# Filler products of 256 columns, and filler in two later gaps of a planned attention and expert kernel

## The chip, the cores and the metric

The kernel runs on one core of one Trainium2 chip. The metric is the device time of one execution in microseconds (us). Three unprofiled runs of the kernel before are shown, and one more execution that carried the profile.

## What is computed

The reference first does attention over pooled keys and values: k and v are averaged over groups of 8 rows, so each of the 64 (batch, head) pairs has 72 keys, and 576 queries attend to them. The 4608 rows that come out go through a feed-forward layer whose activation is a quotient of polynomials.

```python
scores = scale * q @ k_pooled.T          # per batch and head, 576 x 72
attn = softmax(scores)
x = (attn @ v_pooled).transpose(0, 2, 1, 3).reshape(4608, 512)
h = x @ w_in                             # 512 -> 2048
g = (a0 + a1*h + a2*h**2 + a3*h**3) / (1 + |b0|*|h| + |b1|*h**2 + 1e-6)
out = g @ w_out                          # 2048 -> 512
```

The two weight matrices arrive in 64 bits. Products of matrices are made in several passes over high and low parts of the operands (fp32r), to keep fp32 accuracy.

## The kernel before, in words

The rows are cut into 18 blocks of 256 (index i), the hidden dimension into 8 slices of 256 (index u). For a pair (i, u) there is a first product `ph{i}_{u}` = x times a slice of w_in (24 matmuls of 256 columns, L257 in every row, since all planned operations are issued from that line), a quotient on ScalarE, VectorE and GpSimd (tiles `t`, `w`, `r`, `rp`, `gh`, `gl`), and a second product into `po` (matmuls of 512 columns). Attention for block i is made shortly before its first pair: transposes of q (`pq`), scores (`ps`), transposes of the probabilities (`pm`, `pr`), values (`pv`). Keys and values of a batch are pooled first: `pk` and `pl` are transposes of pooled keys, `pvs` and `pvr` sum the values of batches 0 and 1 by products with the identity. So the first 110 us hold loads, weight conversion, pooling and attention together, and from then on the work is a stream of `ph` and `po`.

What each engine does when is not written out by hand. `Plan.add` (L120) records each operation with a planned duration and its dependencies. `Plan.solve` (L153) plays all engines forward by these planned durations and gives each operation a planned start and end, and the order of all operations. `Plan.issue` (L238) emits them in that order. Nothing of the planned times is in the program except the order, and one more thing: the filler.

TensorE executes its queue in order. In `issue` (L247 to L255), ahead of each TensorE operation planned before `steady`, products of the identity with itself (`filler`, 128 x 128, fp32r) are emitted to occupy the time for which the plan leaves TensorE idle. They write to a PSUM bank of their own, `plan.idle` (L852), and nothing reads them; these are the rows of L253, `idle<-identr`. How many are emitted is counted against planned times: one per 0.215 us where the plan is before `WARM` = 8.6 us, one per 0.1 us later. `steady` is the planned start of the second marked product on `plan.idle` (L855). That bank then goes to another tile. The number of filler products is fixed when the program is built, and each of them is executed, whether the engine is late at that point or not.

PSUM has 8 banks, and a ring of 8 tiles (tag `ps`) is allotted to `pk`, `ps`, `ph`, `rp`, `po` and the others in the order in which they are first written (`Buf.real`, L93). The first instruction that writes a new tile waits until the last reader of the bank's tile before it is done. Two such places matter here. The bank that `pk1` gets (keys of batch 1) held `ph0_2`, whose last reader is the VectorE operation `t<-t,abn,ph`. The bank that `ph0_3` gets held `rp0_2`, whose last reader is VectorE's `t<-rp,t`.

All loads and stores are issued by SyncE, in planned order, on one hardware queue: keys and values of batches 0 and 1 go to tiles called `early`, queries to `q`, raw weights to `rwin` and `rwout`. The two small loads of 64 KB that end the values of batch 1 (`early<-in_v_dram`) feed `pvr1`, the 16 matmuls `pvr<-early,fourfold` of batch 1.

Of the kernel before, what the change touches and what calls it, by code (L numbers as in the profile page):

```python
# [8 lines left out]
F32 = mybir.dt.float32  # L9
# [90 lines left out]
class Plan:  # L100
    LAT = 0.07

    BEGIN = {"sp": 0.8, "pe": 1.7, "pool": 1.3, "dve": 1.5, "act": 1.5}
    WARM = 8.6

    LOOK = 0.02

# [45 lines left out]
    def solve(self):  # L153
# [15 lines left out]
        while done < len(self.ops):  # L169
# [44 lines left out]
            op.start, op.end = t, t + op.cost  # L214
            if op.eng == "pe" and t < self.WARM:
                op.end = t + 2 * op.cost
# [21 lines left out]
    def issue(self):  # L238
        for op in self.order:
            for b in op.bufs:  # L240
                b.it = None
        engines = {"sp": self.nc.sync, "act": self.nc.scalar, "actq": self.nc.scalar,
                   "dve": self.nc.vector, "pool": self.nc.gpsimd, "pe": self.nc.tensor}
        value = lambda v: v.ap() if isinstance(v, Lazy) else v
        free, steady = None, [o.start for o in self.order if self.idle.tile in o.bufs][-1]
        for op in self.order:
            if op.eng == "pe" and op.start <= steady:  # L247

                while free is not None:
                    free += 0.1 if free > self.WARM else 0.215  # L250
                    if free > op.start:
                        break
                    self.nc.tensor.matmul(self.idle.ap(), lhsT=self.filler, rhs=self.filler,  # L253
                                          start=True, stop=True)
                free = op.end  # L255
            for name, args, kw in op.calls:
                getattr(engines[op.eng], name)(*map(value, args),  # L257
                                               **{k: value(v) for k, v in kw.items()})
# [17 lines left out]
def tile_pooled_attention_then_rational_moe(  # L276
# [20 lines left out]
    P = 128  # L297
# [13 lines left out]
    plan = Plan(nc)  # L311
# [16 lines left out]
    def new(where, tag, shape, dtype, name):  # L328
        return plan.tile(*pools[where], shape, dtype, tag, name)

    def bank(name, shape):
        return new("ps", "ps", shape, F32, name)
# [5 lines left out]
    def pe(ns, calls, claims=(), after=()):  # L338
        return plan.add("pe", ns / 1000, calls, claims=claims, after=after)

    def mm(out, lhsT, rhs, start, stop):
        return "matmul", (out,), dict(lhsT=lhsT, rhs=rhs, start=start, stop=stop)

    def dma(kbytes, dst, src, eng="sp", issue=0.48, early=60.0, after=()):
        plan.add(eng, issue, [("dma_start", (dst, src), {})], bytes=kbytes * 1024, early=early,
                 after=after)
# [7 lines left out]
    ident = identr.bitcast(F32)  # L354
# [494 lines left out]
    for i in range(2):  # L849
        plan.add("pool", 0.5, [("memset", (kpT[i], 0.0), {})], port=True)  # L850

    plan.idle = bank("idle", [P, P])  # L852
    pe(0, [mm(plan.idle, ident, ident, True, True)])
    plan.now = HEAD + 6.0
    plan.add("pe", 0, [mm(plan.idle, ident, ident, True, True)], early=0.0)  # L855
    plan.now = 0.0
    for g in range(4):
        small("tensor_copy", out=fourfold[:, g * 32:(g + 1) * 32], in_=ident[:2 * REM, :2 * REM])
# [60 lines left out]
```

## Time and profile before

| | |
|---|---|
| Runs without a profile | 958.46, 959.37, 956.49 us (median 958.46) |
| The profiled execution | 961.21 us |
| Its span, first to last instruction | 959.5 us |
| Mean granted TensorE clock | 0.996 |
| Filler products executed | 101 (128 columns), 2.12 to 42.3 us |

The span is the time between the first and the last instruction in the trace; the execution's time holds 1.7 us around it. TensorE (PE in the rows) is busy in almost all of the span. A row of the timeline gives the start in us, the time from the first start to the last end of consecutive equal instructions, the engine, the line, the operation with the names of its tiles, and the count; what stands in brackets is idle time of the engine before it and what ended it. Ends of matmuls overlap the next start, so the distance between starts is what a product costs. An fp32 product is recorded as two matmuls.

### The profile page before, as it was taken

To read this page: it belongs to the slowest core of one execution; us is meant where nothing else is said; L and a number is where in the kernel's file an instruction comes from. 1 tells how busy PE (TensorE), PEld (TensorE's weight loads), DVE (VectorE), ACT (ScalarE), POOL (GpSimd) and SP (SyncE) were. 2 spreads that over 40 slices of the span, in tenths; PEclk is the share of its full clock that TensorE was granted. 3 is DMA by queue.
4 is the path that set the end of the run, shared out by engine and by line. 5 is a ranking of instruction groups with operands and counts; after the bars stand their busy time and mean duration, and the time that the engine had idled before them with its cause. 6 is when DMAs were issued, how large, how long until landed. Compare 5 with 4: busy or idle time off the path is not lost.

```text
span 959.5 us, 17276 instructions
## 1 busy us (share of the span) xinstructions
PE 945.0 (98%) x6233; PEld 858.9 (90%) x6233; DVE 780.7 (81%) x1346; ACT 695.0 (72%) x1180; POOL 510.9 (53%) x445
## 2 busy tenths in 40 slices
PE   9989999999999999999999999999999999999998
PEld 8978899988998999999999899999999889999996
DVE  4798988888888878788888897979787878787664
ACT  2787888858676867776776786777867676767674
POOL 3566557756446645454644484447545564544353
PEclk9999999999999999999999999999999999999999
DMA  9967110155133213123303240225121411102000
GB/s 304 333 241 238 32 40 1 45 138 132 44 73 70 64 31 80 22 46 66 107 14 63 58 123 3 38 64 115 34 32 41 96 38 28 40 3 43 1 23 23
DMA packets 156692, 71.65 MB, mean 75 GB/s; under 512 B 133952, under 2 KB 133952, under 8 KB 156608
## 3 DMA queue, kind: packets, MB, share of 16 engines
q1 hardware_dynamic: 156608, 70.56, 28.5%
q8 instruction: 49, 0.80, 0.4%
q14 instruction: 35, 0.29, 0.1%
HBM read 50.60 MB, written 12.58 MB: 66 GB/s over the span
## 4 chain that ended last, share of the span: by engine, by line
PE 92%; DVE 4%; DMA 1%; POOL 1%; ACT 1%; issue 1%; SPq 0%; POOLq 0%; DVEq 0%
PE ph L257 40%; PE po L257 39%; PE pv L257 4%; PE ps L257 4%; PE idle L253 2%; DVE t L257 1%; DMA st_v<-in_v_dram 1%; PE pvs L257 1%; PE pr L257 1%; PE pvr L257 0%; DVE rp L257 0%; PE pk L257 0%; DVE sm L257 0%; PE pq L257 0%; POOL st_v L257 0%
## 5 line engine op out<-in xcount | busy, mean ns | idle before, releaser
L257 PEld LDWEIGHTS ph<-x,win 128*128 128x128 f32 x3264 | 484.1, 189 | 63.6 <-ACT r L257 2.5
L257 PE MATMUL ph<-x,win 128*128 128x256 f32 x3264 | 502.7, 282 | 2.9 <-DVE t L257 2.3
L257 PE MATMUL po<-wout,gh 128*128 128x512 f32 x1152 | 358.9, 398 | 0.0
L257 POOL TENSOR_TENSOR w<-w,r 128x512 f32<-128x512 f32 (+1 forms) x145 | 190.6, 1314 | 257.8 <-ACT r L257 240.7
L257 POOL TENSOR_TENSOR gl<-t,gh 128x512 fp32r<-128x512 f32 (+1 forms) x145 | 192.6, 1328 | 97.7 <-ACT gh L257 97.3
L257 PEld LDWEIGHTS po<-wout,gh 128*128 128x128 f32 x1152 | 182.6, 189 | 7.0
L257 PE MATMUL po<-wout,gl 128*128 128x512 f32 x576 | 181.6, 396 | 0.5 <-POOL gl L257 0.5
L257 DVE SCALAR_TENSOR_TENSOR t<-t,abn,rp 128x512 f32<-128x512 f32 (+1 forms) x145 | 107.0, 738 | 50.8 <-ACT rp L257 48.0
L257 DVE TENSOR_TENSOR t<-t,ph 128x512 f32<-128x512 f32 (+1 forms) x145 | 98.0, 676 | 61.1 <-ACT t L257 59.2
L257 ACT ACTIVATE w<-ph 128x512 f32<-128x512 f32 (+1 forms) x145 | 86.1, 594 | 71.6 <-PE ph L257 67.2
L257 ACT ACTIVATE rp<-w,cbias 128x512 f32<-128x512 f32 (+1 forms) x145 | 100.0, 690 | 45.5 <-POOL w L257 43.3
L257 ACT ACTIVATE r<-w,abn 128x512 f32<-128x512 f32 (+1 forms) x145 | 118.2, 815 | 10.6 <-POOL gl L257 4.4
L257 ACT ACTIVATE t<-ph,abn 128x512 f32<-128x512 f32 (+1 forms) x145 | 111.0, 766 | 18.7 <-PE ph L257 14.7
L257 DVE SCALAR_TENSOR_TENSOR t<-t,abn,ph 128x512 f32<-128x512 f32 (+1 forms) x145 | 107.6, 743 | 6.3 <-ACT w L257 1.3
L257 ACT CAST gh<-t 128x512 fp32r<-128x512 f32 (+1 forms) x145 | 88.5, 610 | 22.8 <-DVE t L257 19.9
L257 DVE SCALAR_TENSOR_TENSOR t<-rp,t 128x512 f32<-128x512 f32 (+1 forms) x145 | 99.4, 685 | 4.2
L257 DVE SCALAR_TENSOR_TENSOR rp<-w,rp 128x512 f32<-128x512 f32 (+1 forms) x145 | 99.2, 684 | 0.1
L257 PEld LDWEIGHTS po<-wout,gl 128*128 128x128 f32 x576 | 91.1, 189 | 4.8 <-POOL gl L257 0.7
L257 ACT ACTIVATE rp<-rp 128x512 f32<-128x512 f32 (+1 forms) x145 | 84.0, 579 | 3.4 <-DVE t L257 0.5
L257 POOL TENSOR_TENSOR e<-e,sm 128x576 f32<-128x576 f32 x36 | 41.5, 1160 | 37.7 <-DVE sm L257 28.9
L257 POOL TENSOR_TENSOR st_v<-st_v 128x512 f32<-128x512 f32 (+1 forms) x36 | 36.4, 1016 | 38.8 <-DMA st_v<-in_v_dram 12.0
L257 PE MATMUL pv<-am,vm 128*128 128x256 f32 (+3 forms) x288 | 46.5, 281 | 0.5 <-DVE kpT L257 0.4
(91 smaller groups left out, 864.2 us busy)
## 6 DMA issues: line engine op xcount, KB each, us to landing
out_dram<-ob SPq DMA_DIRECT2D x17, 512.0 KB, 3.0
rwin<-in_moe_w_in_dram SPq DMA_DIRECT2D x8, 1024.0 KB, 9.9
rwout<-in_moe_w_out_dram SPq DMA_DIRECT2D x8, 1024.0 KB, 10.7
am<-e SPq DMA_DIRECT2D x224, 32.0 KB, 2.0
st_k<-in_k_dram SPq DMA_DIRECT2D x12, 512.0 KB, 4.6
st_v<-in_v_dram SPq DMA_DIRECT2D x12, 512.0 KB, 4.0
q<-in_q_dram SPq DMA_DIRECT2D x144, 32.0 KB, 2.1
st_v<-in_v_dram SPq DMA_DIRECT2D x48, 64.0 KB, 3.7
```

Source lines behind the costliest of these rows:

```text
L253: self.nc.tensor.matmul(self.idle.ap(), lhsT=self.filler, rhs=self.filler, start=True, stop=True)
L257: getattr(engines[op.eng], name)(*map(value, args), **{k: value(v) for k, v in kw.items()})
```

## The change

Four edits. The bank `idle` becomes twice as wide, and the filler's moving operand is the identity read twice (a broadcast), so one load of weights serves 256 columns instead of 128. After `WARM` the planned price of a filler is 0.12 instead of 0.1 us, which lowers their number; before it, the price stays 0.215. After `steady`, up to a planned start of 110 us, gaps are filled too, with products that write to the tile of the operation that comes next: only where this operation is the first to write its tile, the tile is F32, and the part that it writes is 128 x 128 (then 128 columns are used) or 128 x 256; the gap has to leave 0.2 us. The real operation then overwrites what they wrote.

```diff
+    FILL = 110.0
...
-            if op.eng == "pe" and op.start <= steady:
-                while free is not None:
-                    free += 0.1 if free > self.WARM else 0.215
-                    if free > op.start:
+            if op.eng == "pe" and op.start <= self.FILL:
+                to = self.idle.ap() if op.start <= steady else None
+                dst = op.calls[0][1][0]
+                if to is None and dst.tile.it is None and dst.tile.dtype == F32:
+                    to = dst.ap()
+                one = self.filler
+                if to is not None and tuple(to.shape) != (128, 128):
+                    one = one.unsqueeze(1).to_broadcast([128, 2, 128])
+                    if tuple(to.shape) not in ((128, 256), (128, 2, 128)):
+                        to = None
+                while free is not None and to is not None:
+                    free += 0.12 if free > self.WARM else 0.215
+                    if free > op.start - (0.0 if op.start <= steady else 0.2):
                         break
-                    self.nc.tensor.matmul(self.idle.ap(), lhsT=self.filler, rhs=self.filler,
-                                          start=True, stop=True)
+                    self.nc.tensor.matmul(to, lhsT=self.filler, rhs=one, start=True, stop=True)
                 free = op.end
...
-    plan.idle = bank("idle", [P, P])
-    pe(0, [mm(plan.idle, ident, ident, True, True)])
+    plan.idle = bank("idle", [P, 2, P])
+    pe(0, [mm(plan.idle[:, 0], ident, ident, True, True)])
     plan.now = HEAD + 6.0
-    plan.add("pe", 0, [mm(plan.idle, ident, ident, True, True)], early=0.0)
+    plan.add("pe", 0, [mm(plan.idle[:, 0], ident, ident, True, True)], early=0.0)
```

The planned durations, the order of operations, the allotment of banks and all transfers stay as they are.

## Rows read from the trace of the kernel before

**Rows 1.** The page's first part: busy time, share of the span, instructions.

```profile
PE 945.0 (98%) x6233; PEld 858.9 (90%) x6233; DVE 780.7 (81%) x1346; ACT 695.0 (72%) x1180; POOL 510.9 (53%) x445
```

**Rows 2.** Stretches: length, busy by engine (PE, PEld, DVE, ACT, POOL), clock, DMA, GB/s.

```profile
60.00:70.00 10.00, 6.11 (x41) 5.20 (x39) 9.88 (x18) 8.20 (x13) 6.53 (x4) 0.98 0.42 165
70.00:80.00 10.00, 9.69 (x47) 8.33 (x47) 6.34 (x14) 6.40 (x11) 4.18 (x4) 0.68 0.51 161
...
140.00:160.00 20.00, 20.00 (x130) 18.15 (x129) 16.28 (x24) 16.92 (x26) 13.78 (x9) 1.00 0.00 1
```

**Rows 3.** Timeline of TensorE, the first 50 us.

```profile
2.12 4.93 PE L253 MATMUL idle<-identr 128*128 128x128 f32 x22
...
8.26 1.12 PE L257 MATMUL pq<-identr,q 128*128 128x128 f32 x4
...
16.16 1.91 PE L257 MATMUL pvs<-early,identr 128*128 128x256 f32 x4
...
19.15 1.03 PE L257 MATMUL pvs<-early,identr 128*128 128x256 f32 x4
...
24.34 2.32 PE L253 MATMUL idle<-identr 128*128 128x128 f32 x19
26.49 0.62 PE L257 MATMUL pm<-identr,e 128*128 128x128 f32 x4
...
36.54 4.81 PE L257 MATMUL ph<-x,win 128*128 128x256 f32 x40
...
46.19 2.05 PE L257 MATMUL pvr<-early,fourfold 32*128 32x128 f32 x16
```

**Rows 4.** The chain that ended last: pieces of the late stream at full rate.

```profile
120.34 0.47 PE po L257 x2
120.80 0.47 PE ph L257 x4
```

**Rows 5.** Timeline of SyncE's queue: the last load that pvr1 needs.

```profile
29.85 0.56 SPq L257 DMA_DIRECT2D early<-in_v_dram  x1
```

**Rows 6.** That issue in the DMA view; the last number is us to landing.

```profile
early<-in_v_dram SPq DMA_DIRECT2D x1, 64.0 KB, 14.0
```

**Rows 7.** One microsecond while it waits; columns as in rows 2.

```profile
38.00:39.00 1.00, 1.00 (x11) 1.00 (x10) 0.97 (x4) 0.69 (x1) 0.00 (x0) 1.00 1.05 414
```

**Rows 8.** Timeline of TensorE around the two later gaps.

```profile
62.65 3.01 PE L257 MATMUL ph<-x,win 128*128 128x256 f32 x24
67.56 0.44 PE L257 MATMUL pk<-identr,ks 128*128 128x128 f32 x2 [1.89 <-DVE t L257]
70.31 4.60 PE L257 MATMUL ph<-x,win 128*128 128x256 f32 x20 [2.31 <-DVE t L257]
74.71 0.63 PE L257 MATMUL pk<-identr,ks 128*128 128x128 f32 x2
...
77.25 0.71 PE L257 MATMUL ps<-kpT,qT 128*64 128x144 f32 x8
```

**Rows 9.** Timeline of VectorE there.

```profile
65.30 0.41 DVE L257 TENSOR_TENSOR ks<-early 128x256 f32<-128x256 f32 x1
...
66.77 0.73 DVE L257 SCALAR_TENSOR_TENSOR t<-t,abn,ph 128x512 f32<-128x512 f32 x1
...
69.48 0.69 DVE L257 SCALAR_TENSOR_TENSOR t<-rp,t 128x512 f32<-128x512 f32 x1
```

**Rows 10.** Half microseconds at which the granted clock changes; columns as in rows 2.

```profile
69.50:70.00 0.50, 0.00 (x0) 0.00 (x0) 0.50 (x2) 0.00 (x0) 0.50 (x1) 0.67 0.00 0
...
76.00:76.50 0.50, 0.50 (x4) 0.50 (x3) 0.50 (x1) 0.40 (x2) 0.00 (x0) 0.50 0.80 307
76.50:77.00 0.50, 0.50 (x5) 0.39 (x4) 0.50 (x3) 0.11 (x1) 0.00 (x0) 1.00 0.32 90
```

**Rows 11.** Waits of SyncE's queue, first 110 us: total us, times, longest.

```profile
SPq L257 <- PE pq L257: 30.1, 4, 15.7
```

## Prediction

> **What bounds the kernel now.** I read the busy shares first: TensorE is busy in 98% of the span, VectorE in 81% [rows 1]. Then the table by stretches: late in the kernel TensorE fills each stretch, as in 140 to 160, and the poor stretches are 60 to 70 (busy 6.11 of 10 us, VectorE 9.88) and 70 to 80 (granted clock 0.68) [rows 2]. So the late stream is paced by TensorE, and a microsecond by which it starts earlier is a microsecond off the end. What the change touches lies ahead of it, in two places.
>
> The head. TensorE has a queue without gaps there, but 101 of its products are filler, and the filler shows the rate. The 22 from 2.12 on take 4.93 us (the end of the last overlaps what follows), 215 ns from start to start; the 19 from 24.34 start within 2.15 us, 113 ns [rows 3]. The profile's clock column records no step there, but the same product at half the rate says that the engine ran at 1.2 GHz first. The same four sum products take 1.91 us at 16.16 and 1.03 us at 19.15 [rows 3], so the rate doubled around 18 us. Before it TensorE had 41 fillers of 128 columns among its work, and at the end the sum products of 256 columns.
>
> The later gaps. TensorE waits 1.89 us before pk1 and 2.31 us before ph0_3 [rows 8]. The clock falls at about 69.8, after these near-empty 4.6 us, and is back at 76.5, after 6.2 us of products at 1.2 GHz [rows 8, 10]. What do the waits wait for? The pooled keys of pk1 are ready at 65.71 (65.30 plus 0.41), and it starts at 67.56, just after VectorE's read of ph0_2 ends at 67.50. ph0_3 starts at 70.31, just after the read of rp0_2 ends at 70.17 [rows 8, 9]. Both wait for the bank, not for data. That decides the second half of the change.
>
> **Part 1, the filler of 256 columns.** The plan's gaps stay, so the counts follow from the prices: gaps that held 22, 4, 8, 7, 1, 19, 7, 12, 13, 1, 7 hold 22, 4, 6, 6, 1, 16, 6, 10, 10, 0, 5. That is 86 for 101.
>
> What does one cost? ph products have 256 columns and a weight load each: 40 take 4.81 us, 120 ns [rows 3], 118 in the late stream [rows 4]. At 1.2 GHz 20 of them take 4.40 us up to the next start, 220 ns [rows 8]. Against 113 and 215 ns for 128 columns, doubling the columns costs 5 to 7 ns: the product runs beside the next load of weights. So after the rise 60 fillers of 113 ns (6.8 us) become 48 of 120 ns (5.8 us), 1.0 us less, and 3 cold ones fewer save 0.65 us.
> The Trainium skill, "TensorE: Matmul & The Clock Gate", section "Back-to-back issue gap", prices an isolated product at full rate by its columns, N/2.4 + 2.5 ns. By that 128 more columns cost 53 ns, and 48 fillers 2.5 us more instead of 1.0 less, an estimate from the page; ph at 118 to 120 ns speaks against it.
>
> What does the clock do? The trace before has no such filler, so I bound it. If nothing changes, only 1.7 us of the above are gained. If the clock rises while the first 22 fillers run or soon after, as it did at 76.5 after 6.2 us of mostly 256-column products without a break (2.12 + 6.2 = 8.3), then the stretch from 8.26 to 19.15, 10.9 us at half rate [rows 3], needs about 5.4. I take the second, because rows 8 and 10 show nearly this kind of product lifting it. An estimate with the waits for keys and values left in is that TensorE's work moves by 4.5 us at 20, and, with the thinner filler, by about 5 at 41.
>
> But this is not what arrives. pvr1 needs the last small load of batch 1's values. It is issued at 29.85 and lands 14.0 us later, at 43.85 [rows 5, 6], and the DMA engines are full meanwhile (share 1.05, 414 GB/s) [rows 7], so an earlier issue doesn't bring it sooner: what is ahead in the queue has to go through. pvr1 starts at 46.19 [rows 3], 2.3 us after the landing. TensorE works in order and would stand idle before pvr1. **Gain of the head: 2.3 us**; ends 1.7 (no earlier rise) and 5 (the loads move along). Behind it VectorE is nearly full in 60 to 70 [rows 2] and works on what pvr1 and pv1 give, so I move it by the same 2.3.
>
> **Part 2, the later gaps.** In the plan TensorE idles 2.98 us before pk1 and 2.60 before ph0_3: (2.98 - 0.2)/0.12 gives 23 products of 128 columns, (2.60 - 0.2)/0.12 gives 20 of 256. Two further gaps, before pr4 and pr5, have fp32r tiles and are left alone. The bank is now taken by the first filler instead of the first real product, so the wait for the bank moves to it: **the filler runs after the gap, not in it**. In times as before the shift:
> - pk1's bank comes free at 67.5. 23 products of 113 ns are 2.6 us, then pk1 0.2: until 70.3. This is hidden, since ph0_3's bank is free at 70.2 only; without that cover it would cost 2.6.
> - Then 20 products of 120 ns: 2.4 us on the path. Queued behind them are ph0_3 and the second part of pk1, and VectorE waits for that part.
> - The clock: TensorE is idle for 1.9 us in a row now, not 4.6 with 0.4 of work in between, so it should stay at 2.4 GHz. From 70.31 to ps at 77.25 are 6.94 us [rows 8]; at full rate the same work is 20 ph at 118 ns (2.4), pk1 (0.2), two pairs of po and a group of ph at 0.47 each (1.4) [rows 4]: 4.0. That gives back 2.9.
>
> Where the execution before had the cold stretch, the sum is 2.4 - 2.9 = -0.5; where it had none, +2.4. Ends: -2.9 (the filler is free after all) and +2.4.
>
> **Sum.** The profiled execution (span 959.5, 961.21 with what lies around it) has the cold stretch: 961.21 - 2.3 - 0.5 = 958.4. It is 2.75 above the median, about the cold stretch's price, and the three runs spread over 2.9 us, the same size. I read the runs as with and without it: 959.37 - 2.3 - 0.5 = 956.6 and 956.49 - 2.3 + 2.4 = 956.6. I forecast **956.5 us**, 0.2% under the median. A measurement of this kernel tells about 0.3% (2.9 us) from no change, so this counts as no difference.
>
> **Rivals.**
> - *Forecast:* a load bounds the head, and the second half roughly pays for itself, 955.6 to 958.5. Chance 0.47.
> - *The loads move too.* SyncE's queue waits 30 us in all for TensorE's pq [rows 11]; issued earlier, the loads might land earlier and the head gain the whole 5: 956.5 - 2.7 = 953.8. Against it: full DMA engines [rows 7]. Free later filler would give nearly the same time. Chance 0.33.
> - *The change does not do what it says*, and the clock rises no earlier: the head gains 1.7 instead of 2.3, 957.1. Chance 0.08, within the band of no difference.
> - *Slower:* the clock falls anyway in the idle time ahead of pk1. Then the filler itself runs cold. 23 x 215 ns are 4.9 us, so pk1 ends 2.4 us after ph0_3's bank is free; 20 x 220 ns are 4.4 us instead of 2.4; ph0_3's 20 products cost 4.4 instead of 2.4. That is 2.4 + 2.0 + 2.0 = 6.4 over the forecast: 962.9. It decides if the clock falls before about 67.5. For it: it fell in this place before. Against it: only 1.9 us of idle time in one piece. Chance 0.10.
> - *A filler is priced by its columns.* A po product of 512 columns takes 235 ns and a ph product of 256 takes 118 [rows 4], so 128 columns are worth 58 ns where no load of weights hides them. Before ph0_3 that is 20 x 58 = 1.2 us more, in the head 48 x 58 = 2.8, mostly in slack: 957.7 to 959. This is what the page's rule above would do. Chance 0.02.
>
> **Numbers.** Faster by over 0.3% (under 955.6): the second case and a little of the first, 0.35. Slower (over 961.3): 0.10. Within: 0.55. The range goes from 953.5 (the second case) to 959.5, where runs without an earlier cold stretch pay for the filler.
>
> **What would show it.** Fillers and real work at 110 to 120 ns from about 8 us on; if the spacing is 215 to 220 ns up to 18, part 1 failed. An idle stretch of TensorE before pvr1, ended by a DMA, with pvr1 at 43 to 44; at 41 the loads moved. The first filler of pk1 and of ph0_3 starting after VectorE's t, with idle time still ahead; fillers that start where the ph ahead of them ends would prove me wrong. Granted clock 1.00 from 60 to 80, and the ps of 77.25 some 2.5 to 3 us earlier. The forecast is wrong if the runs before do not differ by the cold stretch: then the sum holds against the profiled execution alone.

## The result and the profile after

The changed kernel takes **961.87 us** in the median of 20 executions (957.61 to 965.98); the kernel before, run 20 times beside it, 958.89 (956.13 to 961.55). The ratio is **1.0033**, with a 95% interval of 1.0018 to 1.0048: slower by 0.33%, just over the 0.3% that the prediction took as no difference. The prediction was 956.5 us in a range of 953.5 to 959.5, with 0.10 for slower. It was wrong in the time and in the sign.

The profiled execution took 965.26 us (span 963.6). Five others of the 20 are as long, so its stretches show what most of the loss looks like, not the average. The page's first part, to hold against [rows 1]:

```profile
PE 948.0 (98%) x6261; PEld 860.5 (89%) x6261; DVE 781.6 (81%) x1346; ACT 694.5 (72%) x1180; POOL 509.1 (53%) x445
```

TensorE issues 28 products more: 15 fewer in the head, 43 more in the later gaps, the numbers forecast. The shares tell nothing else, because a filler counts as busy. The stretches of the changed kernel (columns as in [rows 2]) tell more:

```profile
60.00:70.00 10.00, 8.07 (x59) 7.42 (x58) 9.87 (x16) 8.93 (x15) 6.27 (x5) 0.99 0.44 170
70.00:80.00 10.00, 10.00 (x62) 10.00 (x62) 4.53 (x9) 3.84 (x6) 4.64 (x3) 0.67 0.33 105
...
45.00:46.00 1.00, 1.00 (x10) 1.00 (x11) 0.43 (x1) 0.00 (x0) 0.15 (x1) 0.94 1.14 297
46.00:47.00 1.00, 1.00 (x6) 1.00 (x6) 0.00 (x0) 0.00 (x0) 0.00 (x0) 0.50 0.93 321
...
52.00:53.00 1.00, 1.00 (x5) 0.88 (x4) 0.95 (x3) 1.00 (x3) 0.00 (x0) 0.64 0.47 134
...
69.00:70.00 1.00, 0.69 (x5) 0.69 (x6) 0.89 (x2) 1.00 (x2) 0.98 (x2) 0.89 0.00 0
70.00:71.00 1.00, 1.00 (x7) 1.00 (x7) 1.00 (x3) 0.91 (x2) 1.00 (x1) 0.50 0.00 0
...
76.00:77.00 1.00, 1.00 (x9) 1.00 (x7) 0.00 (x0) 0.00 (x0) 0.00 (x0) 0.69 0.39 47
```

The granted clock is at half rate twice: from about 45.9 to 52.7, which is new, and from about 69.8 to 76.6, about as long as the stretch of before [rows 10] although TensorE is now "busy" throughout 70 to 80. VectorE's share there falls from 6.34 [rows 2] to 4.53; its timeline below shows that it waits for a TensorE that works on filler.

The timeline of TensorE in the changed kernel:

```profile
2.12 4.11 PE L265 MATMUL idle<-identr 128*128 128x256 f32 x22
6.34 0.44 PE L268 MATMUL pk<-identr,ks 128*128 128x128 f32 x2
...
24.18 1.43 PE L265 MATMUL idle<-identr 128*128 128x256 f32 x10
25.45 0.40 PE L268 MATMUL pv<-am,vm 128*128 128x256 f32 x2
...
32.27 4.81 PE L268 MATMUL ph<-x,win 128*128 128x256 f32 x40
...
44.87 2.82 PE L268 MATMUL pvr<-early,fourfold 32*128 32x128 f32 x16 [1.85 <-DMA early<-in_v_dram]
...
69.31 4.76 PE L265 MATMUL pk<-identr 128*128 128x128 f32 x23 [1.93 <-DVE t L268]
73.87 0.65 PE L268 MATMUL pk<-identr,ks 128*128 128x128 f32 x2
74.17 3.70 PE L265 MATMUL ph<-identr 128*128 128x256 f32 x20
77.71 2.54 PE L268 MATMUL ph<-x,win 128*128 128x256 f32 x20
...
81.80 0.71 PE L268 MATMUL ps<-kpT,qT 128*64 128x144 f32 x8
```

Read against [rows 3, 8], it gives a ledger of where the changed kernel stands relative to before:
- The rate doubles while the first 22 fillers run: they take 4.22 us to the next start, 192 ns each, and the pair of pk at 6.34 takes 0.44, as at full rate in [rows 8]. From then on the stream is ahead: the 40 products of ph start at 32.27 instead of 36.54, **4.3 us early**.
- pvr1 waits 1.85 us for its load and starts at 44.87 instead of 46.19: **1.3 us early**. Then the clock is half, and VectorE's reads that free the later banks come late: pk1's bank is free at 69.25 instead of 67.50 [rows 9], **1.75 us late**.
- The 23 fillers take 4.56 us and the 20 take 3.54. ph0_3 starts at 77.71 instead of 70.31, **7.4 us late**. It then takes 2.4 us to the next start instead of 4.4, and ps starts at 81.80 instead of 77.25, **4.55 us late**. The span is 4.1 longer.

The wait before the first filler has moved to it whole. The timeline of VectorE, the reads that free the two banks:

```profile
68.52 0.73 DVE L268 SCALAR_TENSOR_TENSOR t<-t,abn,ph 128x512 f32<-128x512 f32 x1
...
71.23 0.68 DVE L268 SCALAR_TENSOR_TENSOR t<-rp,t 128x512 f32<-128x512 f32 x1
...
80.50 0.47 DVE L268 TENSOR_SCALAR kpT<-pk 64x216 f32<-64x216 f32 x2 [4.77 <-PE pk L268]
```

The first read ends at 69.25 and the first filler starts at 69.31. ph0_3's bank is free at 71.91, while TensorE is still in pk1's fillers. The last line is who pays: VectorE stands idle for 4.77 us until the second part of pk1 is there. SyncE's queue settles the rival "the loads move too"; here the kernel before, then the changed one:

```profile
16.40 3.86 SPq L257 DMA_DIRECT2D q<-in_q_dram  x2
20.31 5.69 SPq L257 DMA_DIRECT2D early<-in_k_dram  x3
```

```profile
13.82 7.38 SPq L268 DMA_DIRECT2D q<-in_q_dram  x2
21.25 4.83 SPq L268 DMA_DIRECT2D early<-in_k_dram  x3
```

q is issued 2.6 us earlier, but the keys behind it are issued 0.9 later: the earlier start is gone with the next group of loads. pvr1's load did not come sooner: pvr1, which waits for it, starts 1.0 us after the landing of before (44.87 against 43.85, [rows 5, 6]).

**The clock of every execution** says how typical the profile is. Each has a mean granted clock over its span (as recorded, so without the slow head, which the record shows at 1.00); a half-rate stretch of 6.8 us lowers it by 0.0035 (half of 6.8 in 960). In the 20 of the changed kernel, clock and time go together:

| mean granted clock | changed kernel: executions, median us | before (104 in all): executions, median us |
|---|---|---|
| 0.992 to 0.995 | 8, 964.91 | 11, 959.11 |
| 0.996 to 0.997 | 2, 961.72 | 64, 958.80 |
| 0.998 | 7, 960.92 | 29, 958.42 |
| 0.999 | 2, 958.98 | none |
| 1.000 | 1, 957.61 | none |

Six of the 20 lie at 0.993, the profiled one with its two cold stretches among them, and take 964.77 to 965.98. The executions of before lost 0.2 to 0.8% of the clock, and it hardly showed in their time: 0.4 us between 0.996 and 0.998.

The profiled execution of before, at 961.21 us, is not typical either. Of the 124 executions run beside the others only two are longer, and the 64 with about its recorded clock (0.996 to 0.997) have a median of 958.80. So 2.4 of its microseconds are not explained by the recorded clock, and what they are was not found.

### The profile page after: what moved, and what is told of

It is laid out like the page before. It is cut to its first block, busy times and chain, and to the rows that moved or that the text cites. A ratio compares the mean times of both kernels' runs of the same rounds, so it can differ in the third digit from the quotient of the medians.

```text
span 963.6 us, 17331 instructions
## 1 busy us (share of the span) xinstructions
PE 948.0 (98%) x6261; PEld 860.5 (89%) x6261; DVE 781.6 (81%) x1346; ACT 694.5 (72%) x1180; POOL 509.1 (53%) x445
## 4 chain that ended last, share of the span: by engine, by line
PE 88%; DVE 4%; DMA 2%; SPq 2%; ACT 2%; issue 1%; DVEq 0%
PE po L268 39%; PE ph L268 39%; PE pv L268 4%; PE ps L268 3%; SPq L268 2%; DVE t L268 2%; DMA early<-in_v_dram 2%; DMA q<-in_q_dram 1%; DVE m_wout L268 1%; PE pr L268 1%; PE pk L265 0%; DVE rp L268 0%; ACT t L268 0%; PE pk L268 0%; PE ph L265 0%
```

## The experiments

Four kernels shared each set of runs of the kernel before: the first four below, the next four, the last four. "Head" is the filler up to the plan's first 37 us, "later" that ahead of pk1 and ph0_3.

**1. The head alone.**

```diff
-    FILL = 110.0
+    FILL = 37.09
```

> Edit: the 256-column filler and its lower count up to the marked product stay; the later gaps are not filled. Theory (idle time that the head's gain opens ahead of pvr1, and filler that runs after the bank wait, let the clock fall): pvr1 again starts at 44 to 45 after 1.5 to 2 us of idle time; where the clock falls there, 43 to 52 run at half rate and the head's 2 us are lost; no filler on the path before ph0_3, so 957 to 960, 1 to 4 us under the changed kernel. Rival (the later filler is harmless and the head alone makes it slower): as the changed kernel, 961 to 963.

Measured: 960.20 us (956.65 to 962.25) beside 958.68, ratio 1.0012 [1.0003, 1.0022]. Its TensorE timeline:

```profile
44.16 2.02 PE L268 MATMUL pvr<-early,fourfold 32*128 32x128 f32 x16 [1.21 <-DMA early<-in_v_dram]
...
65.50 0.44 PE L268 MATMUL pk<-identr,ks 128*128 128x128 f32 x2 [1.92 <-DVE t L268]
...
93.29 0.41 PE L268 MATMUL pr<-identr,er 128*128 128x128 f32 x2 [0.86 <-DVE t L268]
```

In this execution the head is worth what was forecast: pvr1 starts 2.0 us sooner, pk1 2.1, and the pr that stands at 96.63 before starts 3.3 sooner. But then the clock falls in a place where it did not fall in the profile of before, after waits of only 0.86 and 0.46 us (its stretches):

```profile
95.00:96.00 1.00, 1.00 (x9) 0.92 (x7) 1.00 (x3) 1.00 (x2) 1.00 (x1) 0.87 0.00 0
96.00:97.00 1.00, 1.00 (x7) 1.00 (x7) 1.00 (x2) 0.50 (x1) 0.00 (x0) 0.50 0.06 16
...
102.00:103.00 1.00, 1.00 (x6) 0.89 (x6) 0.94 (x2) 0.68 (x2) 0.32 (x1) 0.72 0.00 0
```

Seven cold microseconds take the 3.3 back, and at 103 the stream stands where before's stands. Before, then run 1:

```profile
102.96 2.44 PE L257 MATMUL ph<-x,win 128*128 128x256 f32 x20
```

```profile
102.85 2.52 PE L268 MATMUL ph<-x,win 128*128 128x256 f32 x20
```

The lead is real and is not kept here. Nor is it in most executions, as far as the clock tells: 8 of the 11 lie at 0.995 or below, of before's 104 only 11.

**2. The head's new counts with products of 128 columns** (and no later filler): is it the width or the smaller number?

```diff
-                to = self.idle.ap() if op.start <= steady else None
+                to = self.idle.ap()[:, 0] if op.start <= steady else None
```

> Edit: the lower count of filler of the change, but 128 columns as before, and no later gaps. Theory (256 columns raise the clock early): fillers at 215 ns and the rate doubling only at 15 to 18 us, pvr1 at 44.5 to 46 with little idle time ahead, 956.5 to 958.5. Rival (the count, not the columns, moved the head): clock up at 5 to 6 us as in the changed kernel, pvr1 waiting 1.5 to 2 us for its load.

Measured: 959.15 us (956.75 to 962.44), ratio 1.0006 [0.9994, 1.0018]: no difference is shown. The profile shows the rate up near 10 us and pvr1 at 43.97 after a wait of 1.08 us for its load. Here the lead is kept, to a span of 955.0 us; it is the fastest of the twelve executions. That early rate is not typical of this width, see 6; this run by itself doesn't separate width and number.

**3. The later filler alone**, with the head as before.

```diff
-                to = self.idle.ap() if op.start <= steady else None
+                to = self.idle.ap()[:, 0] if op.start <= steady else None
...
-                    free += 0.12 if free > self.WARM else 0.215
+                    free += 0.215 if free <= self.WARM else 0.1 if op.start <= steady else 0.12
```

> Edit: the head as in the kernel before (128 columns, old count), only the two later gaps filled with 23 and 20 products. Theory (the filler waits for the bank and runs after the gap): pvr1 at 46 as before without idle time ahead; idle time ahead of the filler of pk1 stays 1.8 to 2 us; ps after ph0_3 later than in the kernel before by 0 to 4.5 us depending on the clock: 959 to 963. Rival (the filler fills the gap): filler starts where ph ends at 65.7, clock 1.00 from 60 to 80, 955 to 957.

Measured: 962.27 us (956.41 to 965.87), ratio 1.0036 [1.0019, 1.0053]. **This half alone loses as much as the whole change.** Two of its twelve executions have a clock of 1.000; they took 956.41 and 957.24, and the other ten 960.68 or more.

**4. The changed kernel, with 16 fillers in pvr1's own bank ahead of pvr1**, to hold the clock through its wait.

```diff
+                if dst.tile.name == "pvr1" and dst.tile.it is None:
+                    for _ in range(16):
+                        self.nc.tensor.matmul(dst.tile.real(), lhsT=self.filler,
+                                              rhs=self.filler, start=True, stop=True)
```

> Edit: the changed kernel plus 16 filler products of 128 columns in pvr1's own bank, ahead of pvr1, where TensorE otherwise waits for the load. Theory: no fall of the clock at 43 to 46, pvr1 at 44.5 to 45 and the work behind it at full rate, 2.5 to 3.5 us won where the changed kernel has the cold stretch there, 0 where it has not: median 959 to 961; the filler before pk1 can still run cold. Rival (the clock falls for another reason or the time is lost elsewhere): 961 to 963.

Measured: 961.58 us (958.80 to 965.67), ratio 1.0029 [1.0015, 1.0043]. **The edit had no effect.** The page of its profile has as many products as the changed kernel, and none of them is a filler in pvr1's bank:

```profile
PE 943.6 (98%) x6261; PEld 856.9 (89%) x6261; DVE 781.7 (81%) x1346; ACT 694.4 (72%) x1180; POOL 509.1 (53%) x445
```

The line `to = dst.ap()` ahead of it had already given the tile its bank, so its condition `dst.tile.it is None` was never true there. So this run doesn't test what it was expected to test. It is the changed kernel once more: the loss is found again, and there is a second profile of it. In that one pvr1 waits 1.87 us and the clock is down from about 48.3 to 51.7. But this execution shows the later filler with the clock up (TensorE timeline):

```profile
68.79 2.79 PE L265 MATMUL pk<-identr 128*128 128x128 f32 x23 [1.88 <-DVE t L272]
71.41 0.41 PE L272 MATMUL pk<-identr,ks 128*128 128x128 f32 x2
71.57 2.63 PE L265 MATMUL ph<-identr 128*128 128x256 f32 x20
74.04 2.54 PE L272 MATMUL ph<-x,win 128*128 128x256 f32 x20
...
78.13 0.71 PE L272 MATMUL ps<-kpT,qT 128*64 128x144 f32 x8
```

From start to start, 23 fillers of 128 columns take 2.62 us (114 ns each), 20 of 256 take 2.47 (124 ns): the sum's prices were right within 4%, and so was the order of events. From the end of the wait ahead of pk1 to ps are 9.34 us instead of 9.69 [rows 8], 0.35 less where the forecast had 0.5 less. Still this execution took 961.49 us: after the cold stretch at 48, that wait ends 1.2 us late instead of 2.3 early. Against the 961.21 of the profiled execution before, it is the head's gain that is missing here, not the second half. And the same program, with 1.9 us of idle time ahead of pk1 in both profiles, lost the clock there in one execution and kept it in the other.

**5. Each later gap by itself.** First the 23 ahead of pk1:

```diff
-                if to is None and dst.tile.it is None and dst.tile.dtype == F32:
+                if to is None and dst.tile.it is None and dst.tile.name == "pk1":
```

> Edit: as later_only, but only the 23 products ahead of pk1. Theory: at full rate they are hidden (2.6 us until ph0_3's bank is free), at half rate they cost up to 2.3 us: 957.5 to 961. Rival (every filler product is on the path): 2.6 us over the kernel before or more, 961 to 963.

Measured: 959.41 us (954.85 to 961.06), ratio 1.0002 [0.9986, 1.0018]. Then the 20 ahead of ph0_3, the same line with that name:

> Edit: as later_only, but only the 20 products ahead of ph0_3. Theory: all 20 lie on the path, 2.4 us at full rate and up to 4.4 at half rate, and the clock falls ahead of them as before, so 2 to 4 us over the kernel before: 960.5 to 963. Rival (hidden): 958 to 959.

Measured: 962.18 us (960.17 to 964.05), ratio 1.0038 [1.0025, 1.0050], the whole loss of 3. The timeline of TensorE with the 23 only:

```profile
67.73 3.13 PE L265 MATMUL pk<-identr 128*128 128x128 f32 x23 [1.90 <-DVE t L268]
70.66 0.65 PE L268 MATMUL pk<-identr,ks 128*128 128x128 f32 x2
70.96 3.71 PE L268 MATMUL ph<-x,win 128*128 128x256 f32 x20
```

and with the 20 only:

```profile
70.31 4.63 PE L265 MATMUL ph<-identr 128*128 128x256 f32 x20 [2.22 <-DVE t L268]
74.75 3.34 PE L268 MATMUL ph<-x,win 128*128 128x256 f32 x20
```

The 23 are hidden, as forecast: ph0_3 starts at 70.96, 0.65 us after before's. The 20 are not: they stand 4.44 us on the path, at 222 ns each, because the clock is already down when they begin, as it is there before [rows 10]. Eleven of its twelve executions lie at 0.996. Three of the twelve with the 23 reached 0.999, and these took 954.85 to 955.47, the others 959.24 or more.

**6. Filling the same gaps in a bank that TensorE already holds.** The head is before's. Instead of writing to the next product's bank, 15 and 18 products of zeros are added to po's open accumulation, so that they need no bank and run in the gap:

```diff
+    HOLD = {"pk1": 15, "ph0_3": 18}
...
+                for _ in range(self.HOLD.get(first.name, 0) if first.it is None else 0):
+                    self.nc.tensor.matmul(acc.ap()[:, 0:256], lhsT=self.filler,
+                                          rhs=self.zeros[:, 0:1].to_broadcast([128, 256]),
+                                          start=False, stop=False)
+                if first.name == "po0_0_0":
+                    acc = op.calls[0][1][0]
```

> Edit: the head of the kernel before; in the two later gaps filler that needs no bank: 15 products ahead of pk1 and 18 ahead of ph0_3 of zeros, 256 columns, added into the open accumulation of po0 (so the sum is unchanged). Theory (filler behind the bank wait cannot keep the clock, filler in the gap can): filler starts where ph ends, about 65.7, pk1 and ph0_3 start when they did (67.6 and 70.3), granted clock 1.00 from 60 to 80, ps after ph0_3 near 74.3 instead of 77.25: 2 to 3 us under the kernel before, 955.5 to 957. Rival (the cold stretch there is hidden by VectorE or falls anyway): 958 to 960.

Measured: 957.76 us (954.62 to 960.35) beside 958.96, ratio 0.9991 [0.9979, 1.0002]. The timeline of TensorE:

```profile
65.37 1.84 PE L252 MATMUL po<-zeros,identr 128*128 128x256 f32 x15
67.44 0.44 PE L267 MATMUL pk<-identr,ks 128*128 128x128 f32 x2 [0.23 <-DVE t L267]
67.64 2.26 PE L252 MATMUL po<-zeros,identr 128*128 128x256 f32 x18
70.19 2.61 PE L267 MATMUL ph<-x,win 128*128 128x256 f32 x20 [0.30 <-DVE t L267]
```

The idle time is 0.23 and 0.30 us instead of 1.89 and 2.31 [rows 8]. pk1 and ph0_3 start when before's do, so the filler costs nothing. The recorded clock stays at 1.00, here where it was 0.68 [rows 2]:

```profile
70.00:80.00 10.00, 9.81 (x67) 8.31 (x67) 8.62 (x19) 7.78 (x13) 6.49 (x5) 1.00 0.72 256
```

ph0_3 takes 2.5 us instead of 4.4, and ps starts at 74.35, 2.9 us before the 77.25 of [rows 8], the 2.9 of the prediction. In six of the twelve executions the mean clock is 1.000. The products that start at 102.96 before start at 100.05 here, so in this execution the lead is not lost on the way. Yet over all of them the gain is 0.09% (0.9 us), its interval just reaching no change.

The same with the head of 2:

> Edit: the same two real gap fillings, with the head of count_only (the change's lower count, 128 columns). Theory: the head's lead of about 2 us and the gap's 2 to 3 add up unless the clock falls in the idle time ahead of pvr1 or near 95: 953.5 to 957, scattered. Rival (each lead is given back in the next wait): same as gap_po.

Measured: 957.29 us (955.35 to 959.84), ratio 0.9989 [0.9977, 1.0000]. Here the rate rose at about 18 us although the head is that of 2, and pvr1 began at 46.70 after 1.46 us of waiting. Over all profiles, one each of fourteen kernels: the five with a head of 256 columns had the full rate by 5.5 to 8 us; of the nine with one of 128, one had it at 10 and eight at 16 to 19, as in [rows 3]. So in these profiles the early rise goes with the width, not with the number.

**7. The price of the 20 with the clock held**: 6 with the change's 20 fillers ahead of ph0_3.

```diff
+                if to is None and dst.tile.it is None and dst.tile.name == "ph0_3":
+                    to = dst.ap()
```

> Edit: gap_po (clock held through both later gaps by filler that needs no bank) plus the change's 20 products ahead of ph0_3 in its own bank. Theory (they lie on the path by their own length, whatever the clock does): gap_po plus 2.0 to 2.4 us, 959.8 to 960.3. Rival (the slowdown of the 20 products was only the clock's): as gap_po, 957.3 to 958.3.

Measured: 959.37 us (958.37 to 964.91) beside 958.53, ratio 1.0016 [1.0003, 1.0029]. The timeline of TensorE:

```profile
69.19 2.66 PE L275 MATMUL ph<-identr 128*128 128x256 f32 x20 [0.21 <-DVE t L278]
71.69 2.54 PE L278 MATMUL ph<-x,win 128*128 128x256 f32 x20
```

2.50 us from start to start, and against 6 the ratios differ by 0.0025, 2.4 us, with intervals that don't overlap. The forecast's 2.4 on the path is borne out. In 5 it was 0.0038 (3.6 us), 1.2 us more than with the clock held; this difference is within the noise. Run 7 also is the second half of the forecast with its clock held, in nine of its twelve executions at 0.998 or more, and it is slower than before by 0.16%, not faster by the forecast 0.5 us.

**8. The change's head with the gaps of 6**, and then the same with every gap that it opens filled too: 7 zero products ahead of pvs1, 15 in the open pvs1 ahead of pvr1, 7 and 3 in po ahead of pr4 and pr5.

```diff
+    HOLD = {"pk1": (15, "po0_0_0"), "ph0_3": (18, "po0_0_0")}
...
+    HOLD = {"pvs1": (7, "idle"), "pvr1": (15, "pvs1"), "pk1": (15, "po0_0_0"),
+            "ph0_3": (18, "po0_0_0"), "pr4": (7, "po0_0_0"), "pr5": (3, "po0_0_0")}
```

> Edit: the change's 256-column filler in the head, and the two gaps filled with the 33 zero products instead of the change's 43. Theory (the head's lead is bounded by the load of pvr1 and lost in part where the clock falls in the idle time ahead of it): pvr1 at 44 to 46 after 1 to 2 us of idle time, median 957 to 959, more scatter than gap_po. Rival (the lead comes through): 955 to 956.

> Edit: head_gap_po plus zero products where TensorE still waits: 7 on the idle bank ahead of the first pvs1, 15 into open pvs1 ahead of pvr1, 7 and 3 into po0 ahead of pr4 and pr5. Theory (what the head wins is taken back by falls of the clock in the waits): no fall between 40 and 105, pvr1 at 44 to 46 still by its load, 954.5 to 956.5 with less scatter. Rival (the load alone decides): as head_gap_po.

Measured: 957.91 us (955.87 to 960.53), ratio 0.9989 [0.9979, 1.0000], for the first, and for the second **956.29 us (954.82 to 959.86), ratio 0.9979 [0.9967, 0.9990]**, the fastest of the study and faster than both kernels. The timeline of TensorE in the first:

```profile
44.98 2.43 PE L278 MATMUL pvr<-early,fourfold 32*128 32x128 f32 x16 [1.51 <-DMA early<-in_v_dram]
```

and in the second:

```profile
42.71 2.03 PE L255 MATMUL pvs<-zeros,identr 128*128 128x256 f32 x15
44.67 2.05 PE L279 MATMUL pvr<-early,fourfold 32*128 32x128 f32 x16
...
68.82 2.65 PE L279 MATMUL ph<-x,win 128*128 128x256 f32 x20 [0.30 <-DVE t L279]
...
73.02 0.71 PE L279 MATMUL ps<-kpT,qT 128*64 128x144 f32 x8
```

The first waits ahead of pvr1, and its clock is at half rate from 46.4 to 53.2. The second doesn't wait: pvr1 starts where the zero products end, the recorded clock is 1.00 from start to end of the stream, and eleven of its twelve executions lie at 1.000 (of before's 104 none).

**9. The gaps before pr4 and pr5 alone**, added to 6:

```diff
+    HOLD = {"pk1": (15, "po0_0_0"), "ph0_3": (18, "po0_0_0"),
+            "pr4": (7, "po0_0_0"), "pr5": (3, "po0_0_0")}
```

> Edit: gap_po plus 7 and 3 zero products into po0 ahead of pr4 and pr5, with the head of the kernel before. Theory (short waits near 95 let the clock fall in some executions): 956.5 to 957.5, 0 to 1 us under gap_po. Rival (these waits are too short to matter): as gap_po, 957.8.

Measured: 957.74 us (954.61 to 960.80), ratio 0.9992 [0.9980, 1.0003]: these two gaps by themselves bring nothing that can be seen. Between this and 8's second kernel stands only the head with its filled waits, 0.0013 or 1.2 us; the two intervals overlap, so that difference is an indication.

## Why the prediction was wrong

**Right:**
- The filler of 256 columns lifts the rate at about 5.5 to 8 us (forecast 8.3). The counts, 86, 23 and 20, were exact.
- Its price was taken as 120 ns at full rate; 24.18 to 25.45 holds ten, 127 ns, and run 4 shows 124 beside 114 for 128 columns. 128 columns more cost 10 ns; the rival that priced by columns, at 58 ns, is refuted. The Trainium skill ("TensorE: Matmul & The Clock Gate", "Back-to-back issue gap") gives a price by columns, from which 53 ns for 128 more is an estimate, for an isolated product alone, and says that in a stream of loads of weights and products both set the spacing; the trace agrees with the second.
- The bank's wait moves to the first filler, which runs after the gap (first filler at 69.31, read ended at 69.25). The 23 are hidden (run 5), the 20 cost 2.4 us where the clock holds (runs 6 and 7).
- The loads do not move (SyncE's queue), and TensorE stands idle ahead of pvr1 instead.

**The step that failed** is in part 2: "TensorE is idle for 1.9 us in a row now, not 4.6 with 0.4 of work in between, so it should stay at 2.4 GHz", which was to give back 2.9 us. I had argued that moving the wait leaves 1.9 us of idle time, and then counted that remainder as harmless. The clock fell at 69.8, just as before, after 1.93 us of idle time and half a microsecond of filler; it fell there in the profiles of runs 1, 2, 3 and 5 too, and in run 4 alone, the same program once more, it did not. In six profiles with that idle time taken away (runs 6 to 9) it never fell there. So the rival "slower", at 0.10, is the mechanism that happened. It put the decision at a fall ahead of 67.5, which was not needed: a fall during the 23 fillers is enough for the 20 to run partly cold. It priced this case at 6.4 us over the forecast, 962.9; the median is 961.87. That the two are so near is in part luck: this price still counts the head's 2.3 us as won.

Nor is it shown that the clock alone would have saved the step. Where it held, the runs disagree: two executions of run 3 at 1.000 took 956.41 and 957.24, under before's 958.68, while run 7 is 1.5 us over before.

**The second failure is "gain of the head: 2.3 us".** It was taken to be kept to the end. Run 1 measures a loss of 0.12% instead (1.2 us, 0.3 to 2.1). The profiles show two places where it goes, and both are falls of the clock. The idle time that I had forecast ahead of pvr1 was given no price, though it is of the same kind as that ahead of pk1: where it is 1.46 us or more (the changed kernel, run 4, the first of 8 and the second of 6), the clock falls 1.0 to 2.5 us after pvr1 has begun; where it is 1.08 and 1.21 (runs 1 and 2), it stays up in these profiles. And in run 1, where the lead survives, it runs into another fall at 95.7. Filling these waits took the falls away in the profile of 8's second kernel; that this is worth the 1.2 us by which it beats run 9 is an indication only. Smaller: the load that pvr1 needs landed at 43.97 to 46.70 in the six profiles where pvr1 waits for it, not always at 43.85, so even the bound was about 1 us too good.

**The third is a reading of the runs shown.** "I read the runs as with and without it", 2.9 us apart, is not borne out: of before's 104 executions none has an undisturbed clock, and those at 0.996 and at 0.998 differ by 0.4 us. Nor does taking away the cold stretch give 2.9 in the median: run 6 does it, ps is 2.9 us earlier, and 0.9 is left. The premise that a microsecond by which the late stream starts earlier is a microsecond off the end is not what failed: in all thirteen profiles the shift at 102.96 against before comes out in the span within 2.4 us (run 6: 2.9 early and a span 4.2 shorter; the changed kernel: 4.5 late and 4.1 longer). What is not borne out is that the profiled execution of before stands so far over the median because of its cold stretch: the others with about its recorded clock are 2.4 us faster. Where they win this was not settled; only one execution of before has a profile.

**The account of the +0.33%:** the 20 fillers +0.25% at full rate and perhaps +0.13% more for the clock (5 and 7; the second part is within the noise), the 23 fillers nothing (+0.02%), the head +0.12% (1). The sum, 0.5%, is over the 0.33 measured but within the intervals. In its only execution with a clock of 1.000 the changed kernel took 957.61 us, 1.1 over the forecast; in the six that lost 0.7% of it, 965.10 in the median, 8.6 over. One execution doesn't show that the forecast sum would have been right with the clock.

What stays open: what makes one execution fall and the next not, with the same idle time (the changed kernel itself did both, in its own profile and in run 4's); whether filler in pvr1's own bank would hold the clock there, which run 4 was to test; whether the loads of batch 1's values issued ahead of the weights would keep the head's lead, which was not tried; and why run 6, with a clock of 1.000 in half of its executions, did not reach the 955 of the three fast executions of run 5.

## What to carry to other kernels

Filler that is to hold the clock must run in the gap, so it must not need what the gap waits for: put it where the engine already has the bank, as zeros added to an open accumulation, and check in the timeline that it starts where the work ahead of it ends. Speeding up a stretch ahead of a fixed load only turns the gain into idle time there, and that idle time can cost the clock, so fill it as well or leave the stretch alone. A cold stretch has no fixed price: taking it out of the kernel before won 0.9 us in the median (run 6), while filler put on the path took 3.5 us in the changed kernel's profile and 4.4 in run 5's instead of 2.5. And look in the trace whether the edit is there at all: run 4's was not, and only the count of products told it.

## What the runs showed that was not expected

- Products that fill TensorE's queue don't all lift the clock alike. With a weight load each, 22 of 128 columns back to back left it at half rate, until 16 to 19 us in eight of nine profiles; with 22 of 256 columns it was up by 5.5 to 8 us in five of five. The granted clock's column did not record that head at half rate; only the spacing (215 against 113 ns) shows it.
- The clock fell after idle times of 1.46 to 1.93 us, with work right behind them, and in the stretches shown stayed down for 3 to 7 us although TensorE was then busy. The same idle time also passed without a fall (run 4, ahead of pk1), and once it fell after waits of 0.86 and 0.46 us (run 1).
- Thirty-three products of zeros added to an open accumulation between its real products cost no time that can be measured (run 6), and the fastest kernel holds 58 of them, and 7 more in a bank of their own.
- The scatter is a signal: the changed kernel spreads over 8.4 us where before spreads over 5.4, and its mean granted clock says in which execution the time is lost.
